# Attention and a mixture of experts in one program: a pick of the largest expert partly on GpSimd, two copies on ScalarE, clears later, one drain moved, rows turned in other steps

## The chip, the cores and the metric

The kernel runs on one core of a Trainium2 chip. Its time is the device time of one execution in microseconds (us). PE is TensorE, ACT ScalarE, DVE VectorE, POOL GpSimd, SP SyncE.

## The reference

`q`, `k`, `v` are 8 batches x 8 heads x 576 positions x 64. Heads 0 to 3 attend to the last 32 positions, heads 4 to 7 to every fourth of the last 128. The result, 4608 tokens of 512 numbers, goes through a mixture of 16 experts in 4 groups; a token belongs to one expert, its two softmax weights scale what the expert gives.

```python
attn = np.exp(scores - scores.max(-1)); attn /= attn.sum(-1) + 1e-9
x = np.matmul(attn, v).transpose(0, 2, 1, 3).reshape(4608, 512)
g_idx = np.argmax(x @ w_group, axis=1)          # group, then expert in it
e_idx = np.argmax(xg @ w_expert[g], axis=1)
h = np.maximum(xg[mask_e] @ w1[g, e], 0.0)      # 512 -> 1024
out[tok_idx] = combined[:, None] * (h @ w2[g, e])   # 1024 -> 512
```

## The kernel before

**Attention and routing.** The attention runs in 36 steps, each on 128 rows of `x` (two batches' share of 64 positions), as a pipeline over 40 loop steps `s`: scores of `s`, values (`av`, L339) and normalisation (L367, L371) of `s - 3`, transposes of `s - 4` for the gates. Values are needed in two places of partitions, so POOL copies half tiles of 64x1040 float32 (`shift_v`, L153 and L157: two a step, for the step after). Between these parts the loop spends a budget of time on a queue of routing work: `route(n)` for a pair of batches (nine steps each) finds each token's expert, its rank among the expert's tokens (`rk`, `slots`, `hl`), its softmax weight (sums on POOL, L462 to L468, then `val`, `parts`) and enters it in a table on PE (`bank`, from `mv`, L535 and L542). `base` holds the running count of tokens for each expert.

After the third and the fourth pair of batches (`AFTER = (2, 3)` indexes them from `base`) `pick(0)` and `pick(1)` choose the expert with the most tokens so far, by the index `ordi`, so that its weights can be loaded and three pieces of its work (EARLY) can begin inside the attention. A pick is seven or eight DVE operations: `cnt` (L585), `key`, (for the second: `key` less the first), `km`, `top`, `kk`, `km`, `ordi` (L607). SP reads `ordi` from memory (L959) and addresses the weights with it. Rows for the early pieces are gathered by POOL (L777) into `xe`, which is cleared first (L1060).

**Main loop.** After the attention there are 16 pieces of rows, sizes 186, 150, 368, 302, 300, 298, ..., 188. For a piece, `k` = 0 to 7 are the first layer's eight column blocks (L869 on PE; `hh` on ACT, L876; `hl` on DVE, L877: each value is split into two float16 numbers, and three products are added), `k` from 8 on the second layer's half tiles of up to 128 rows (L928; `yr` on ACT, L902, scattered by POOL, L889). The first layer writes `a` into four banks of PSUM in turn: block 4 of a piece waits until `hl` of block 0 has read its bank. All engines work in the order in which the loop is written. Within a step `k` that order is the step's own matmuls, `hh` and `hl`; then lists of later pieces (`LISTS`: rows of a piece from the table, L760 to L715); then gathers (`ask_ahead`, by `P2_ASKS` in piece 2; POOL, L801, four quarters for a tile of 128 rows); then the drain; then a turn; then a chunk of the weights of the piece after next (`split`: ACT `wh`, L681, DVE `wl`, L678).

A turn (`turner`) transposes one tile of gathered rows on DVE (`xt`, L822) and splits the one before into `xh` (ACT, L835) and `xl` (DVE, L836). It begins piece `j` only when the loop is one piece behind it, or two behind and past step 9, and a tile only LEAD = 6 steps after it was asked for. Turns come at odd `k` above 2. `xr` has five buffers.

**Drains.** `nc.gpsimd.drain()` (L1273) makes POOL wait for the transfers it has started; it stands in piece 2 at `k` = 12 and in each later piece at `k` = 5, 14 in all.

Of the kernel before, what the change touches and what calls it, by code (L numbers as in the profile page):

```python
# [8 lines left out]
F32 = mybir.dt.float32  # L9
# [4 lines left out]
ALU = mybir.AluOpType  # L14
AX = mybir.AxisListType
PSUM = bass.MemoryType.PSUM

P = 128
# [4 lines left out]
NE = 16  # L23
# [24 lines left out]
DEEP = 3  # L48
NXR = 5
LEAD = 6  # L50
P2_ASKS = (0, 2, 4, 6, 9, 11)
LISTS = {(1, 7): [3], (2, 4): [4], (2, 9): [5]}
NWST = 6
NWST2 = 1
BUDGET = (1.4, 1.4, 2.4, 1.8)
# [17 lines left out]
def moe_attention_kernel(ctx, tc, q, k, v, cmask, wgate, wpack, out):  # L73
# [76 lines left out]
    def shift_v(n):  # L150
        vs[n] = vp[n % NVS]
        odd, even = slice(0, 64), slice(64, P)
        nc.gpsimd.tensor_scalar(vs[n][even], vt[n][even], 1.0, 1.0, ALU.mult, ALU.mult)  # L153
        if n % NJ == 0:
            nc.gpsimd.memset(vs[n][odd], 0.0)
        else:
            nc.gpsimd.tensor_scalar(vs[n][odd], vt[n - 1][odd], 1.0, 1.0, ALU.mult, ALU.mult)  # L157
# [26 lines left out]
    pri = cp.tile([P, 4], F32, name="pri")  # L184
    base = [cp.tile([P, NE], F32, name="base0")] + [None] * NBP
    low = cp.tile([P, P], F32, name="low")
    iota = low[:, 0:MAXOV]
    oob = {4: cp.tile([P, 1], F32, name="oob4"), 2: cp.tile([P, 1], F32, name="oob2")}
    capt = cp.tile([P, NE], F32, name="capt")
# [17 lines left out]
    def iota_of(t, pattern, base, mult):  # L207
        nc.gpsimd.iota(t, pattern=pattern, base=base, channel_multiplier=mult, allow_small_or_imprecise_dtypes=True)

    def setup(part):  # L210
        if part == 0:
            nc.vector.memset(ones, 1.0)
            nc.gpsimd.affine_select(
                out=upper, in_=ones, pattern=[[1, P]], compare_op=ALU.is_gt, fill=0.0, base=0, channel_multiplier=-1
            )
            nc.sync.dma_start(wgr, wgate)
            iota_of(pri, [[-1, 4]], 4, 0)
            iota_of(base[0], [[REG, NE]], 0, 0)
            iota_of(low, [[1, P]], 0, 0)
        if part == 1:  # L220
            iota_of(high, [[REG // P, NE], [1, NK4]], 0, 0)
            nc.vector.tensor_scalar(high, high, float(P), HUGE, ALU.mult, ALU.add)
            nc.scalar.copy(high_ps, high.rearrange("p e k -> p (e k)"))
            nc.scalar.copy(pri_ps, pri)
            nc.vector.memset(E16, 0.0)
            nc.vector.memset(tab[:, 0], 0.0)
            nc.vector.memset(tab[:, 1], 2.0 * NTOK)
            nc.vector.memset(tab[:, 2], 2.0 * NTOK + 1.0)
            ids = wgr[:, 128:].rearrange("p (h v t) -> p h t v", h=2, v=2)
            nc.vector.tensor_copy(val[:, :, 1:3], ids[:, 0])  # L230
            nc.vector.tensor_copy(parts[:, :, 1:3], ids[:, 1])
        if part == 2:
            nc.gpsimd.memset(xe[0][0], 0.0)
            nc.sync.dma_start(xd[NTOK : NTOK + 1, :], xe[0][0][0:1, :])
        if part == 3:
            for j in range(4):
                nc.gpsimd.memset(odd[Q4 * j : Q4 * j + Q4], float(j % 2))
            for g, t in oob.items():
                for i in range(g):
                    nc.gpsimd.memset(t[P // g * i : P // g * i + P // g], float(g * NTOK + i))  # L240
            for r in range(NE):
                nc.vector.memset(capt[:, r : r + 1], float(CAPS[r]))
# [340 lines left out]
    def count(pairs):  # L583
        cnt = sm.tile([P, NE], F32, name="cnt")
        nc.vector.tensor_tensor(cnt, base[pairs], base[0], ALU.subtract)  # L585
        return cnt

    def pick(r):
        T = lambda nm, shape, dt=F32: sm.tile([P] + shape, dt, name=nm)
        cnt = count(AFTER[r])  # L590
        yield 0
        key = T("key", [NE])
        nc.vector.scalar_tensor_tensor(key, cnt, float(NE), iota[:, 0:NE], ALU.mult, ALU.subtract)
        yield 0
        for i in range(r):
            nc.vector.scalar_tensor_tensor(key, top[:, i], -float(NE * NTOK), key, ALU.mult, ALU.add)
            yield 0
        km, kk = T("km", [1]), T("kk", [NE])
        nc.vector.tensor_reduce(km, key, axis=AX.X, op=ALU.max)
        yield 0  # L600
        nc.vector.tensor_tensor(top[:, r], key, km.broadcast_to([P, NE]), ALU.is_equal)
        yield 0
        nc.vector.tensor_tensor(kk, top[:, r], iota[:, 0:NE], ALU.mult)
        yield 0
        nc.vector.tensor_reduce(km, kk, axis=AX.X, op=ALU.add)
        yield 0
        nc.vector.tensor_copy(ordi[:, r : r + 1], km)  # L607
        picked.append(r)
        yield 0

    def settle(i):
        r, off, n, pairs = EARLY[i]
# [369 lines left out]

    def early_slots():
        for i, (_, _, _, pairs) in enumerate(EARLY):
            while i not in found:
                yield
            for t in range(NET[i]):
                fetch_rows(xe[i][t], ente[i], t, pairs * TPB * P)
            yield
# [15 lines left out]
    for s in range(NT + 4):  # L1005
        ripe = bool(gate)
        step_now[0] = s
        if s < NT:
            scores(s)
        if 0 <= s - 3 < NT:  # L1010
            av(s - 3)
        if s < NT:
            softexp(s)
        if 0 <= s - 3 < NT:
            if ripe:
                gate.clear()
            normalise(s - 3)
        if start:
            n = start.pop()
            routes.append(route(n))  # L1020
            next(routes[-1])
            if len(routes) == 1:
                gate.append(1)
            for i, (_, _, _, pairs) in enumerate(EARLY):
                if pairs == n + 1:
                    routes.append(settle(i))
        left = spend(BUDGET[min(max(s - 4, 0) // NJ, NBP) - 1])
        if s % 2 == 0:
            load_q(s + 4)
        if s == 0:  # L1030
            load_k(4, 0)
        if s != 1:
            load_k(s + 4 - s % 2, s % 2 if s else 1)
        if s % 2 == 1 or s == 0:
            load_v(s + 2 + s % 2)
        if 0 <= s - 3 < NT:
            store(s - 3)
        if 0 <= s - 4 < NT:
            transpose_x(s - 4)
        if 0 <= s - 1 < NT:  # L1040
            transpose_p(s - 1)
        if left:
            spend(left)
        flush()
        if s < NT - 1:
            shift_v(s + 1)
        if 2 <= s <= 8 and s % 2 == 0:
            setup(s // 2 - 1)
        for r in picked:
            if r not in ev:  # L1050
                expert(r)
        if 0 in ev and not wq:
            wq.append(prefetch())
        if s == NT - 1:
            keep.close()
            fe = pool("fe", side="right", reuse_waits="tile")
            for i in range(1, len(EARLY)):
                xe[i] = [fe.tile([P, DM], F32, name=f"xe{i}{t}") for t in range(NET[i])]
                for t in xe[i]:
                    nc.gpsimd.memset(t, 0.0)  # L1060
            room = fe.tile([P, 48 * P], F16, name="room")
            cut = lambda a, c: room[:, a * P : (a + c) * P].rearrange("p (c n) -> p c n", c=c)
            for i in range(2):
                xs, hs_ = (cut(24 * i, 4), cut(24 * i + 4, 4)), (cut(24 * i + 8, 8), cut(24 * i + 16, 8))
                eb.append([early(i, xs, lambda hs_=hs_: hs_)])
        if eb:
            run(eb[0], EARLY_STEPS.get(s, 0))
        run(wq)
        if s >= 4 and (s - 4) % NJ == NJ - 1:
            bp = (s - 4) // NJ  # L1070
            if bp < NBP - 1:
                start.append(bp)
        run(eq)
    while routes:
        run(routes)
# [115 lines left out]
    def ask(n, got):  # L1191
        for _ in range(min(n, len(got[4]))):
            got[4].pop(0)()
            held_rows[0] += 1
            asked[id(got[2]), len(got[2]) - 1] = slot[0]

    def begin(got):
        ent, cs, xrs, tq, _ = got
# [46 lines left out]
    def turner():  # L1245
        def ripe(xrs, t):
            return len(xrs) > t and (now[2] or slot[0] >= asked[id(xrs), t] + LEAD)

        for j in range(1, len(pieces)):
            while len(known) <= j or j > now[0] + 1 and (j > now[0] + 2 or now[1] < 9):  # L1250
                yield
            got = begin(known[j])
            yield from spread_quarters(got[3], got[2], pieces[j][2], ripe)
            built[j] = got

    turn = [turner()]
    for i, (r, off, cap) in enumerate(pieces):
# [6 lines left out]
        for k, _ in enumerate(ffn(wsets[r % 2], xs, ent, cs, cap, new_h, tq=tq)):  # L1264
# [4 lines left out]
                    known_next(0)  # L1269
            if k in P2_ASKS if i == 2 else i > 2 and (k in (1, 3, 5) or k == 11 and nt(pieces[min(i + 3, NE - 1)][2]) > 2):  # L1270
                ask_ahead()
            if i > 1 and k == (12 if i == 2 else 5):
                nc.gpsimd.drain()  # L1273
            if k % 2 and k > 2:
                run(turn)
            k0, steps = (0, 8) if k < 8 else (8, 2 * nsel)
            if k == 0:
# [114 lines left out]
```

## Time and profile before

| | us |
|---|---|
| median of 3 runs (lowest, highest) | 573.03 (572.88, 574.16) |
| profiled execution, whole | 575.0 |
| its span on the core | 573.3 |
| PE busy | 541.6 (94%) |
| DVE busy | 428.3 (75%) |
| ACT busy | 331.7 (58%) |
| POOL busy | 325.4 (57%) |

A row of a timeline gives the start, the duration, the engine, the line, the operation with what it writes and reads, and in brackets how long the engine was idle before it and what ended that. In the windows view the number in brackets behind a busy time counts instructions, and PEclk is the share of PE's full clock that was granted. The profiled execution lies 1.7 us over its span and 2.0 us over the median.

### The profile page before, as it was taken

Reading aid. Unit: us, or ns where it says so; the run is one execution under the profiler, and the core shown is the slowest. Engines: PE = TensorE matmul, PEld = TensorE weight load, DVE = VectorE, ACT = ScalarE, POOL = GpSimd, SP = SyncE. Lnnn points to the kernel's source line nnn. Section 1 sums busy time; section 2 is a strip of 40 time slices with the busy share of each in tenths; the row PEclk is TensorE's granted clock in tenths of the full one; section 3 lists DMA queues with packets and bytes.
Section 4 is the critical chain, followed back from the end, with each engine's and each line's share of the span. In section 5 each row is a group of like instructions: output and inputs, shape, how many; then the busy total and the mean of one; then the engine's idle time right before and its main releaser. Section 6 shows DMA issues by size and latency. Waiting matters only on the chain.

```text
span 573.3 us, 16182 instructions
## 1 busy us (share of the span) xinstructions
PE 541.6 (94%) x6340; PEld 382.8 (67%) x6340; DVE 428.3 (75%) x870; ACT 331.7 (58%) x656; POOL 325.4 (57%) x332
## 2 busy tenths in 40 slices
PE   4999999898899999999997999999999999999995
PEld 2787877676767777554665566665756756766873
DVE  5775987889789916985958786978889879777710
ACT  7465685875856426845545456466765756755521
POOL 2795686645565861287476684574646646645011
PEclk9899999998999999999997999999999999999999
DMA  7999887994683453785656775857778678778110
GB/s 218 359 297 332 280 293 252 320 326 127 227 293 98 166 221 116 242 276 176 190 159 200 237 223 177 269 173 231 225 233 256 204 260 273 230 244 286 36 32 30
DMA packets 45824, 125.90 MB, mean 220 GB/s; under 512 B 7693, under 2 KB 8595, under 8 KB 45746
## 3 DMA queue, kind: packets, MB, share of 16 engines
q1 hardware_dynamic: 37506, 105.36, 56.7%
q0 software_dynamic: 8240, 19.48, 9.7%
q8 instruction: 51, 0.84, 0.6%
q14 instruction: 27, 0.22, 0.1%
HBM read 105.93 MB, written 19.22 MB: 218 GB/s over the span
## 4 chain that ended last, share of the span: by engine, by line
PE 57%; DVE 7%; issue 3%; POOL 2%; ACT 1%; DMA 1%; POOLq 0%; DVEq 0%; ACTq 0%
PE a L869 29%; PE y L928 28%; DVE wa2l L678 1%; DVE xt L822 1%; DVE hl L877 1%; DVE xl L836 1%; DMA xr<-xd,sentq 1%; POOL xe L777 1%; DVE wa1l L678 1%; POOL xr L801 1%; DVE wb1l L678 0%; PE pt L850 0%; ACT yr L902 0%; ACT off L270 0%; DVE mv L542 0%
## 5 line engine op out<-in xcount | busy, mean ns | idle before, releaser
L801 POOL DMA_INDIRECT xr<-xd,sentq x129 | 159.4, 1236 | 39.5 <-issue 33.6
L928 PEld LDWEIGHTS <-hh 128*128 128x128 f16 (+14 forms) x960 | 67.2, 99 | 61.5 <-issue 5.0
L889 POOL DMA_INDIRECT out<-yr,sent x30 | 34.2, 1141 | 113.8 <-ACT yr L902 28.4
L877 DVE SCALAR_TENSOR_TENSOR hl<-a,hh 128x256 f16<-128x256 f32 (+14 forms) x136 | 55.2, 420 | 33.3 <-ACT hh L876 33.1
L902 ACT ACTIVATE yr<-y,cs 128x512 f32<-128x512 f32 (+4 forms) x30 | 20.6, 687 | 100.1 <-PE y L928 54.3
L869 PE MATMUL a<-xh,wb1h 128*128 128x256 f16 (+7 forms) x288 | 76.7, 270 | 1.1 <-ACT xh L835 1.1
L869 PE MATMUL a<-xl,wb1h 128*128 128x256 f16 (+7 forms) x288 | 76.6, 270 | 0.2 <-DVE xl L836 0.2
L869 PE MATMUL a<-xh,wb1l 128*128 128x256 f16 (+7 forms) x288 | 76.6, 270 | 0.0
L876 ACT ACTIVATE hh<-a 128x256 f16<-128x256 f32 (+14 forms) x136 | 51.4, 382 | 41.2 <-PE a L869 40.3
L869 PE MATMUL a<-xh,wa1h 128*128 128x186 f16 (+7 forms) x256 | 72.1, 282 | 3.0 <-DVE hl L877 3.0
L869 PE MATMUL a<-xl,wa1h 128*128 128x186 f16 (+7 forms) x256 | 72.0, 282 | 0.3 <-DVE xl L836 0.3
L869 PE MATMUL a<-xh,wa1l 128*128 128x186 f16 (+7 forms) x256 | 71.9, 281 | 0.0
L869 PEld LDWEIGHTS <-wa1h 128*128 128x128 f16 x640 | 59.6, 99 | 15.6 <-issue 3.5
L869 PEld LDWEIGHTS <-wb1h 128*128 128x128 f16 x576 | 54.2, 98 | 11.0 <-issue 1.6
L928 PE MATMUL y<-wb2h,hl 128*128 128x512 f16 (+7 forms) x272 | 59.4, 304 | 1.1 <-DVE hl L877 1.1
L928 PE MATMUL y<-wb2h,hh 128*128 128x512 f16 (+7 forms) x272 | 59.5, 305 | 0.0
L928 PE MATMUL y<-wb2l,hh 128*128 128x512 f16 (+7 forms) x272 | 59.4, 304 | 0.0
L928 PE MATMUL y<-wa2h,hh 128*128 128x512 f16 (+7 forms) x208 | 56.7, 331 | 0.0
L928 PE MATMUL y<-wa2l,hh 128*128 128x512 f16 (+7 forms) x208 | 56.6, 330 | 0.0
L928 PE MATMUL y<-wa2h,hl 128*128 128x512 f16 (+7 forms) x208 | 56.6, 330 | 0.0
L153 POOL TENSOR_SCALAR vs<-v 64x1040 f32<-64x1040 f32 x36 | 38.7, 1088 | 30.5 <-DMA v<-v 18.2
L928 PEld LDWEIGHTS <-hl 128*128 128x128 f16 (+14 forms) x480 | 34.3, 99 | 28.7 <-DVE hl L877 2.0
(218 smaller groups left out, 1271.7 us busy)
## 6 DMA issues: line engine op xcount, KB each, us to landing
w<-wpack SPq DMA_DIRECT2D x128, 512.0 KB, 4.2
v<-v SPq DMA_DIRECT2D x36, 260.0 KB, 5.7
kr<-k SPq DMA_DIRECT2D x34, 256.0 KB, 5.6
qb<-q SPq DMA_DIRECT2D x17, 512.0 KB, 6.0
xd<-x SPq DMA_DIRECT2D x32, 256.0 KB, 4.4
xr<-xd,sentq POOLq DMA_INDIRECT x129, 4.7
xd<-x SPq DMA_DIRECT2D x8, 128.0 KB
qb<-q SPq DMA_DIRECT2D x2, 256.0 KB, 3.3
```

The source lines that it names most:

```text
L153: nc.gpsimd.tensor_scalar(vs[n][even], vt[n][even], 1.0, 1.0, ALU.mult, ALU.mult)
L678: nc.vector.scalar_tensor_tensor(l, staged.pop((r, i - 1)), SW, h, ALU.mult, ALU.subtract)
L777: nc.gpsimd.indirect_dma_start(out=xr[:, 256 * h : 256 * h + 256], out_offset=None, in_=xd[0:known].rearrange("n (h c) -> (n h) c", h=2), ...
L801: nc.gpsimd.indirect_dma_start(out=xr[:, T], out_offset=None, in_=xd.rearrange("n (g c) -> (n g) c", g=4), in_offset=bass.IndirectOffsetOn ...
L822: nc.vector.transpose(xt, xrs[t][:, 0:m].rearrange("p t (d c) -> p t c d", c=4))
L836: nc.vector.tensor_tensor(l, xt, h, ALU.subtract)
L869: nc.tensor.matmul(a[:, 0:cap], ww[:, c * FF + f * P : c * FF + f * P + P], xx[:, c, 0:cap], start=(i == 0), stop=(i == len(mm) - 1),)
L876: nc.scalar.activation(hh[:, f, 0:cap], a[:, 0:cap], AF.Relu)
L877: nc.vector.scalar_tensor_tensor(hl[:, f, 0:cap], a[:, 0:cap], 0.0, hh[:, f, 0:cap], ALU.max, ALU.subtract)
L889: ins = nc.gpsimd.indirect_dma_start(out=out.rearrange("n (g c) -> (n g) c", g=g), out_offset=bass.IndirectOffsetOnAxis(ap=at, axis=0), in ...
L902: nc.scalar.activation(yr[0:n, :], yp[0:n, :], AF.Copy, scale=cs[0:n, t : t + 1])
L928: nc.tensor.matmul(yp[P // g * j : P // g * j + n, 0 : DM // g], h[:, f, t * P : t * P + n], ww[:, f * DM + DM // g * j : f * DM + DM // g ...
```

## The change

The pick leaves out `cnt`: `key` is formed from `base` and a constant `origin` that POOL makes at setup. `kk` and the sum over it become six POOL operations (`place`), queued with the sums of the softmax (`posts`, run by `flush` at a step's end, or by `spend`). Values of steps 32 and 33 are copied by ACT, ahead of the exponential of the same step, not by POOL at the end of the step before. The clears of `xe` for the second and third early piece, and their gathers, come from step 37 on. In the main loop pieces 0 and 2 have turns in other steps, piece 2 may begin at step 8 of piece 0, and the tail row tile that is asked for at the very beginning counts as asked `LEAD` steps earlier; the lists of piece 3 come at step 6 of piece 0 and not at step 7 of piece 1. The drain of piece 2, step 12, goes to piece 1, step 2.

```diff
+TURNS = {0: (1, 3, 5, 8, 9, 10, 11), 2: (3, 5, 7, 8, 9, 10, 11, 12, 13)}
-LISTS = {(1, 7): [3], (2, 4): [4], (2, 9): [5]}
+VS_ACT = (32, 33)
+DRAINS = {1: 2}
+LISTS = {(0, 6): [3], (2, 4): [4], (2, 9): [5]}
...
+        if n in VS_ACT:
+            nc.scalar.copy(vs[n][even], vt[n][even])
+            nc.scalar.copy(vs[n][odd], vt[n - 1][odd])
+            return
...
+            nc.gpsimd.tensor_scalar(origin, base[0], float(NE), None, ALU.mult)
+            nc.gpsimd.tensor_tensor(origin, origin, iota[:, 0:NE], ALU.add)
...
-        cnt = count(AFTER[r])
-        nc.vector.scalar_tensor_tensor(key, cnt, float(NE), iota[:, 0:NE], ALU.mult, ALU.subtract)
+        nc.vector.scalar_tensor_tensor(key, base[AFTER[r]], float(NE), origin, ALU.mult, ALU.subtract)
...
-        nc.vector.tensor_tensor(kk, top[:, r], iota[:, 0:NE], ALU.mult)
-        nc.vector.tensor_reduce(km, kk, axis=AX.X, op=ALU.add)
-        nc.vector.tensor_copy(ordi[:, r : r + 1], km)
+        posts.append(lambda: place(r))
+    def place(r):
+        kk = sm.tile([P, NE], F32, name="kk")
+        nc.gpsimd.tensor_tensor(kk, top[:, r], iota[:, 0:NE], ALU.mult)
+        h = NE
+        while h > 1:
+            h //= 2
+            nc.gpsimd.tensor_tensor(kk[:, 0:h], kk[:, 0:h], kk[:, h : 2 * h], ALU.add)
+        nc.gpsimd.tensor_copy(ordi[:, r : r + 1], kk[:, 0:1])
...
-            while i not in found:
+            while i not in found or i and step_now[0] < NT + 1:
...
+        if s in VS_ACT:
+            shift_v(s)
-        if s < NT - 1:
+        if s < NT - 1 and s + 1 not in VS_ACT:
             shift_v(s + 1)
-                for t in xe[i]:
-                    nc.gpsimd.memset(t, 0.0)
+        if s == NT + 1:
+            for t in xe[1] + xe[2]:
+                nc.gpsimd.memset(t, 0.0)
...
-            asked[id(got[2]), len(got[2]) - 1] = slot[0]
+            asked[id(got[2]), len(got[2]) - 1] = slot[0] or -LEAD
-            while len(known) <= j or j > now[0] + 1 and (j > now[0] + 2 or now[1] < 9):
+            while len(known) <= j or j > now[0] + 1 and (j > now[0] + 2 or now[1] < (8 if j == 2 else 9)):
-            if i > 1 and k == (12 if i == 2 else 5):
+            if k == DRAINS.get(i, 5 if i > 2 else -1):
                 nc.gpsimd.drain()
-            if k % 2 and k > 2:
+            if k in TURNS.get(i, ()) or i not in TURNS and k % 2 and k > 2:
                 run(turn)
```

## Rows read from the trace of the kernel before

**Rows 1.** Windows: stretch, length, busy us (xinstructions) by engine, PEclk, DMA share, GB/s.

```profile
320.00:559.00 239.00, 239.00 (x2037) 164.00 (x2036) 183.84 (x315) 139.72 (x238) 127.10 (x102) 1.00 0.65 209
132.11:134.30 2.19, 2.19 (x41) 1.86 (x41) 1.75 (x7) 1.53 (x5) 1.78 (x2) 1.00 0.01 4
137.72:141.29 3.57, 3.57 (x41) 3.12 (x41) 3.54 (x5) 2.06 (x6) 3.24 (x6) 0.52 0.66 162
146.48:149.17 2.69, 1.43 (x37) 1.13 (x37) 0.64 (x2) 2.66 (x9) 2.69 (x7) 1.00 0.55 122
296.75:303.03 6.28, 6.28 (x51) 4.67 (x51) 2.27 (x3) 1.82 (x3) 2.88 (x3) 1.00 0.33 117
306.26:315.31 9.05, 9.05 (x49) 5.93 (x49) 7.50 (x17) 4.46 (x8) 7.15 (x7) 0.69 0.88 284
```

**Rows 2.** Waits of PE: line, releaser, us in total, times, longest us.

```profile
PE o L339 <- DVE x L371: 5.2, 6, 1.4
PE a L869 <- DVE hl L877: 3.0, 1, 3.0
...
PE o L339 <- DVE hl L509: 2.1, 1, 2.1
PE bank L561 <- POOL mv L535: 1.3, 1, 1.3
PE a L869 <- ACT xh L835: 1.1, 1, 1.1
PE y L928 <- DVE hl L877: 1.1, 2, 0.5
```

**Rows 3.** The line of the drains: duration ns min/median/max, first and last start.

```profile
L1273 POOLq DRAIN  x14: 3977/14164/16655, 267.8 to 551.5; - x14
```

**Rows 4.** Timeline of POOL, 258 to 310 us: start, us, operation, idle before it.

```profile
283.62 1.32 POOL L889 DMA_INDIRECT out<-yr,sent  x1 [6.23 <-ACT wa2h L681]
```

**Rows 5.** Chain of waits, 265 to 310 us: start, us, what.

```profile
296.64 3.99 DMA xr<-xd,sentq
```

**Rows 6.** Timeline of DVE, 258 to 310 us.

```profile
300.76 1.10 DVE L822 STREAM_TRANSPOSE xt<-xr 128x512 f32<-128x512 f32 x1 [5.29 <-DMA xr<-xd,sentq]
```

**Rows 7.** Timeline of ACT, 199 to 240 us.

```profile
221.07 0.69 ACT L902 ACTIVATE yr<-y,cs 128x512 f32<-128x512 f32 x1 [3.44 <-issue]
...
221.84 2.00 ACT L681 ACTIVATE wa1h<-w 128x1024 f16<-128x1024 f32 x2
...
225.90 0.48 ACT L876 ACTIVATE hh<-a 128x150 f16<-128x150 f32 x2
...
228.87 0.62 ACT L835 CAST xh<-xt 128x512 f16<-128x512 f32 x1
```

**Rows 8.** Timeline of DVE, 199 to 240 us.

```profile
226.60 0.54 DVE L877 SCALAR_TENSOR_TENSOR hl<-a,hh 128x150 f16<-128x150 f32 x2
```

**Rows 9.** Timeline of POOL, 199 to 242 us.

```profile
237.93 0.98 POOL L889 DMA_INDIRECT out<-yr,sent  x1 [11.88 <-DVE three L738]
```

**Rows 10.** Timeline of DVE, 125 to 150 us.

```profile
132.47 0.83 DVE L585 TENSOR_TENSOR cnt<-base,base 128x16 f32<-128x16 f32 x1 [0.27 <-ACT base L499]
...
134.22 0.17 DVE L603 TENSOR_TENSOR kk<-top,low 128x16 f32<-128x16 f32 x1
```

**Rows 11.** Timeline of POOL, 125 to 150 us.

```profile
132.23 1.05 POOL L153 TENSOR_SCALAR vs<-v 64x1040 f32<-64x1040 f32 x1 [5.08 <-DMA xe<-xd,ente]
...
141.42 0.20 POOL L467 TENSOR_TENSOR se<-sc 128x9 f32<-128x9 f32 x1
...
147.09 1.44 POOL L1060 MEMSET xe<- 128x512 f32 x3
148.51 1.17 POOL L535 TENSOR_TENSOR mv<-ohh,parts 128x256 f16<-128x256 f32 x2
```

**Rows 12.** Timeline of ACT, 125 to 150 us.

```profile
131.11 0.66 ACT L322 ACTIVATE p<-d 128x512 f32<-128x512 f32 x1 [2.14 <-DVE d L316]
```

**Rows 13.** Timeline of PE, 130.5 to 150 us.

```profile
133.81 0.60 PE L329 MATMUL t<-id,p 128*128 128x128 f32 x4
```

More of the change, by code (lines that the diff above doesn't have):

```diff
@@ L186, in moe_attention_kernel @@
     low = cp.tile([P, P], F32, name="low")
+    origin = cp.tile([P, NE], F32, name="origin")
     iota = low[:, 0:MAXOV]
@@ L589, in pick @@
         T = lambda nm, shape, dt=F32: sm.tile([P] + shape, dt, name=nm)
-        cnt = count(AFTER[r])
-        yield 0
-        key = T("key", [NE])
-        nc.vector.scalar_tensor_tensor(key, cnt, float(NE), iota[:, 0:NE], ALU.mult, ALU.subtract)
+        key, km = T("key", [NE]), T("km", [1])
+        nc.vector.scalar_tensor_tensor(key, base[AFTER[r]], float(NE), origin, ALU.mult, ALU.subtract)
         yield 0
@@ L597, in pick @@
             yield 0
-        km, kk = T("km", [1]), T("kk", [NE])
         nc.vector.tensor_reduce(km, key, axis=AX.X, op=ALU.max)
@@ L601, in pick @@
         nc.vector.tensor_tensor(top[:, r], key, km.broadcast_to([P, NE]), ALU.is_equal)
+        posts.append(lambda: place(r))
         yield 0
-        nc.vector.tensor_tensor(kk, top[:, r], iota[:, 0:NE], ALU.mult)
-        yield 0
-        nc.vector.tensor_reduce(km, kk, axis=AX.X, op=ALU.add)
-        yield 0
-        nc.vector.tensor_copy(ordi[:, r : r + 1], km)
+    def place(r):
[6 more added lines that the diff above has]
+        nc.gpsimd.tensor_copy(ordi[:, r : r + 1], kk[:, 0:1])
         picked.append(r)
-        yield 0
     def settle(i):
```

## The prediction

> **What bounds the kernel now.** I read the windows view first. PE is the bound: from 320 to 559 us it is busy in all of the 239.00 us [rows 1], and no other engine comes near. So a change can only take away what PE idles before that stretch, and the time at half its clock, and what is saved there is kept to the end, because after 320 us PE waits for nobody. The waits of PE come second [rows 2]: 3.0 us in the main loop for `hl`, 1.1 for `xh`, twice about 0.55 for `hl` in the second layer; in the attention 2.1 us for `hl` (L509), 1.3 for the table (`bank` after `mv`), and six waits of at most 1.4 us for `x`. The windows around the two longest show the third thing. The 41 matmuls after the 2.08 us wait took 3.57 us at a granted clock of 0.52; the same 41 of the step before took 2.19 at 1.00. A first layer after the 3.02 us wait took 9.05 us at 0.69, where the stretch with as many matmuls ahead of that wait took 6.28 at 1.00. So a long wait of PE here costs itself and then 1.4 or 2.8 us more at the lower of the two levels (1.2 and not 2.4 GHz). After the wait of 1.42 us at 146.48 the clock stayed at 1.00 [rows 1]. The timelines come last, for each wait in turn: who is late, and what it stood behind.
>
> **The drain.** The 3.02 us wait ended at 306.26 with `hl` of piece 4, and DVE was late with that because, in its written order, it stood before `xt` of piece 5 from 295.47 to 300.76, idle 5.29 us [rows 6]. The rows it waited for came by a gather issued at 296.64 that took 3.99 us to land, at 300.63 [rows 5]. That gather is one of a row of gathers that POOL issues nearly without a pause from 283.62 on, and before 283.62 POOL sat idle for 6.23 us [rows 4]: that is where the drain of piece 2, step 12, stands (the drains' first start is 267.8 [rows 3]). The scatter behind it used rows that had been ready long before. With the drain gone POOL goes on at 277.39, up to 6.2 us sooner, and the rows land at 294.4. DVE comes there at 295.47, so its wait goes with 1.1 us to spare, and PE needs only 3.02 of the 5.29 us. Term: 3.0 and 2.8 us of clock, **-5.8**. Nothing that the gathers need is late: their lists are made by step 9 of piece 2, and the buffers of `xr` come free with transposes of piece 3 and the first of piece 4, long written by then.
>
> Where the drain goes, in piece 1, step 2 (about 224 us), POOL has nothing to do: its next instruction is at 237.93 after 11.88 us idle [rows 9]. Behind it stand that scatter and piece 3's gathers. The 14 drains took 4.0 to 16.7 us, 14.2 in the middle [rows 3], most of that with gathers queued ahead; here one or two scatters are ahead. I take 0; the upper bound (16.7 us, to 241) would make the scatter 3 us late, which I treat under the rivals.
>
> **Turns sooner, pieces 0 and 2.** In piece 2 the turns at 7, 8, 9, 10, ... bring `xh` and `xl` of piece 3 ahead of the last `yr` on ACT; before, they stood behind it. The 1.1 us wait for `xh` at the start of piece 3 goes: **-1.1**. DVE will stand waiting in the same piece for rows that have not landed at step 8, but PE needs nothing from it there: all `hl` of piece 2 are done by then.
>
> In piece 0 the transposes and halves of piece 2 (three `xt`, 1.10 us each as at 300.76 [rows 6], and three `xl`) and the lists of piece 3 leave piece 1, where DVE was full and PE waited twice for `hl`: **-1.1**. They go to the second half of piece 0, where DVE has room. But ACT has them in order too. With turns at 8, 9, 10, 11 the three `xh` are written behind steps 9, 10 and 11, so all of them behind `yr`, which waits for PE and runs at 221.07 [rows 7]. In before ACT did after it a short `xh`, three chunks of weights (two took 2.00 us) and two tail outputs, and came to `hh` of piece 1, block 0, at 225.90; `hl` followed at 226.60 [rows 8]. Now three `xh` of 0.62 us [rows 7] replace the short one, 1.9 us for some 0.2 (an estimate: a quarter of the columns, a third of 0.62): `hh` comes 1.7 us later, `hl` too. Block 4 writes the bank that this `hl` frees; PE took block 4 up right behind it in before, with no slack. So a new wait: **+1.7** (1.4 if the `xh` overlap by 0.1 each as ACT's rows do; 2.3 if DVE's chunks push `hl` further by half a chunk). It lies between 1.42 us, after which the clock stayed, and 2.08, after which 1.4 us were lost, so I add half of that: **+0.7**.
>
> **The attention.** `pick(1)` on DVE loses `cnt`, 0.83 us, and `kk`, `km`, `ordi`, 0.17 each by `kk` [rows 10]: 1.3 us in all. They lie directly ahead of the 2.08 us wait, so it would shrink to some 0.7, below 1.42, and the 1.4 us of clock after it go as well. The rule that speaks against the size of this: the Trainium skill, SBUF — State Buffer, section Who interferes with whom, says that a DVE instruction with two inputs in SBUF and a GpSimd instruction that reads SBUF exclude each other. The trace agrees: `cnt` ended at 133.30, POOL's copy at 133.28 [rows 10, 11], and `kk` of the same size took 0.17. By that rule the wait of 0.66 us passes to `key`, which now has two inputs in SBUF, if POOL copies at that moment, and this term would be 0.7 and not 1.3, and with the half that I count below the forecast 0.3 us higher.
>
> The six POOL operations of `place` cost 0.20 us each by the adds of the softmax [rows 11], 1.2 us a pick and the pauses between them. POOL has them free: at 132.23 it had been idle for 5.08 us. SP reads `ordi` after them; the copies that stood there are gone, so I take 0 (bounds 0 and 1.2 a pick).
>
> The copies on ACT: the trace has no 64x1040 float32 copy on ACT. The nearest rows are 1.0 us for 128x1024 (two in 2.00) and 0.69 for 128x512 with a float32 result [rows 7], which doubled is 1.4 us. So 2.1 to 2.8 us a step, ahead of the exponential `p`. ACT was idle 2.14 us before `p` at 131.11 [rows 12], and the transposes that need `p` began at 133.81 [rows 13], 2.0 us after it ended. I take 0; with no cover it would be 2.1 a step. On POOL the copies had waited 5.08 us for a gather to land [rows 11], and the sums, `mv` and the table came late behind them. The clears (1.44 us) stood directly ahead of `mv` at 148.51, for which PE waited 1.3 us [rows 2, 11]; with both gone so should be that wait.
>
> That is 1.3 + 1.4 + 1.3 = 4.0 us at most. But PE waits for `x` in six other places, 5.2 us together [rows 2], so DVE is nearly full here, and the routing and the weights' halves all come one step sooner into it. What is saved in one step is likely to be waited for in the next. I take half, **-2.0** (ends -4.0 and 0).
>
> **Sum:** -5.8 - 1.1 - 1.1 + 1.7 + 0.7 - 2.0 = -7.6. From the profiled execution's 575.0 that is 567.4. The median lies 2.0 us under the profiled execution, so I forecast **565.4** as median against 573.03, 1.3% faster. 0.2% of this kernel (1.15 us) is about what a measurement can tell from none.
>
> **Rivals.**
> - *The attention gives it all.* -4.0 and not -2.0, and no loss of clock in piece 1: 565.4 - 2.0 - 0.7 = 562.7. For it: the waits named end with exactly the operations removed. Against: six waits for `x` beside them. Chance 0.15.
> - *The wait only moves.* In piece 1 2.3 us and the full 1.4 of clock, in the attention 0: 565.4 + 0.6 + 0.7 + 2.0 = 568.7. For it: ACT's order in piece 0 as worked out. Chance 0.15.
> - *The drain's gain does not come:* POOL's gathers wait for something else in that stretch (buffers, lists), `xt` still stands until about 300, the 3.0 and the 2.8 us remain: 571.2. Against: POOL's idle stretch of 6.23 us ends just after the drain and nothing else stands there. Chance 0.08.
> - *Slower: the drain blocks where it now stands.* If it waits for more than the last scatters, POOL's stream from 237.93 on starts late, and with it the gathers of pieces 3, 4 and 5, one behind the other. The 6.2 us gained at 277 take up the lateness: 1.1 us are spare before DVE waits, 2.3 more (5.29 less 3.02) before PE does. So from an end of the drain at 237.9 + 3.4 = 241.3 each us goes to PE. To lose the 7.6 us and 1.4 more it would have to end at 250.3, 26 us after its start, against at most 16.7 seen [rows 3, 9]: 574.4. Chance 0.04.
> - My forecast, 564 to 567: 0.58.
>
> Range: from 561.7 (the first rival less 1.0 for a shorter wait in piece 1) to 569.7 (the second and 1.0 for the copies on ACT); the last two rivals lie outside. Faster by more than 0.2%: 0.91 (all but the slow rival and half of the third); within 0.2%: 0.05; slower: 0.04.
>
> **What would show it.** Right: no wait of PE of 3 us near 300 and a granted clock of 1.00 there; no drain between 240 and 290 and POOL without a pause of 6 us; no `xh` wait at the start of piece 3; a wait of 1.4 to 2.3 us for `hl` in piece 1 at its fifth block; `cnt` gone, and the 2.08 us wait under 1.42 without the 0.52 window. Wrong: `xt` of piece 5 still waiting some 5 us; ACT's copies ending after 133 with PE waiting for `p`; a half clock at a new place, above all where a wait of 2 us or more arises, which would take back 1.4 to 2.8 us each.

## The result and the profile after

The changed kernel took 565.68 us (4 runs, 564.63 to 566.65) against 572.95 of the kernel before: ratio 0.9871, 95% interval 0.9829 to 0.9913. In a later series it was 565.29 against 572.69, 0.9868 (0.9826 to 0.9910). The forecast was 565.4 (561.7 to 569.7). The experiments were run in four series. In two of them the kernel before took 584 to 588 us, and each profiled execution has PE idle for 6 to 16 us that the profile puts to no wait; the times of these two, called the disturbed series below, are given, but carry no part of the account.

The profiled execution took 566.15 us, its span is 564.4, 8.86 less than that of before. Where the time went can be read from PE's timeline: the starts of the first matmul of each piece's first layer (and of DVE's `x` of step 20, which comes before both picks; of the change only the 0.5 us of POOL that make `origin` lie ahead of it), taken from the timelines of the two kernels and subtracted.

| stretch | before, us | after, us | difference |
|---|---|---|---|
| start to `x` of step 20 | 93.21 | 92.56 | -0.65 |
| to piece 0 (the rest of the attention) | 114.43 | 112.16 | -2.27 |
| piece 0 | 16.01 | 16.01 | 0.00 |
| piece 1 | 14.66 | 16.70 | +2.04 |
| piece 2 | 32.27 | 30.51 | -1.76 |
| piece 3 | 26.17 | 25.83 | -0.34 |
| piece 4 | 31.59 | 25.76 | -5.83 |
| all behind it | 244.94 | 244.89 | -0.05 |

The sum is -8.86. The first row is a spread between executions: it lay between -2.0 and +1.2 in the undisturbed ones profiled below, so that medians and not single executions tell the total.

The windows of after that answer to [rows 1] (stretch, length, busy by engine, PEclk, DMA share, GB/s):

```profile
136.46:140.10 3.64, 3.64 (x52) 2.78 (x55) 3.44 (x9) 3.30 (x11) 3.06 (x5) 0.67 0.86 249
225.90:230.00 4.10, 4.05 (x38) 4.05 (x38) 3.87 (x8) 2.33 (x6) 0.00 (x0) 0.58 0.91 304
293.85:300.20 6.35, 6.35 (x53) 4.72 (x52) 6.05 (x13) 4.35 (x8) 3.98 (x4) 1.00 0.82 257
320.00:550.00 230.00, 230.00 (x1956) 158.63 (x1956) 177.73 (x308) 134.18 (x231) 125.27 (x100) 1.00 0.67 212
```

The stretch at the start of piece 4 now takes 6.35 us at 1.00, where the first layer took 9.05 at 0.69; PE still never idles behind 320. Two stretches stand at 0.67 and 0.58 of the clock, both at the lower of the two levels for a part of them: one in the attention, where before had 0.52 behind its wait of 2.08 us, and a new one in piece 1. They follow the two longest waits that PE has behind the first loads, in the list that answers to [rows 2]:

```profile
PE o L349 <- DVE val L525: 2.9, 1, 2.9
...
PE a L880 <- DVE hl L888: 1.8, 1, 1.8
PE bank L571 <- ACT den L359: 1.5, 2, 1.2
PE bank L571 <- ACT ohl L281: 1.0, 1, 1.0
PE tx L410 <- DVE x L381: 0.8, 1, 0.8
PE o L349 <- DVE x L381: 0.8, 2, 0.6
```

The 3.0 us wait for `hl` of piece 4 and the 1.1 for `xh` are gone, and so is the wait for `mv`. Of the waits for `x`, 5.2 us in before, 0.8 are left, and the transposes (`tx`) now wait 0.8 for it. A wait of 1.8 us for `hl` is new; it is the one that the prediction set at 1.7.

POOL, to be laid beside [rows 4, 9], then the drains as in [rows 3], the first of them by itself below, then DVE where piece 5's rows are transposed, as in [rows 6]:

```profile
237.05 0.98 POOL L900 DMA_INDIRECT out<-yr,sent  x1 [12.25 <-ACT yr L913]
...
275.71 1.02 POOL L900 DMA_INDIRECT out<-yr,sent  x1 [0.30 <-ACT csq L737]
277.04 1.39 POOL L812 DMA_INDIRECT xr<-xd,sentq  x1 [0.30 <-issue]
```

```profile
L1287 POOLq DRAIN  x14: 3966/13322/14715, 222.6 to 542.7; - x14
L1287 POOLq DRAIN  x1: 7034/7034/7034, 222.6 to 222.6; - x1
```

```profile
290.62 1.18 DVE L689 SCALAR_TENSOR_TENSOR wb1l<-w,wb1h 128x1024 f16<-128x1024 f32 x1
291.72 1.11 DVE L833 STREAM_TRANSPOSE xt<-xr 128x512 f32<-128x512 f32 x1
```

Between 258 and 291 POOL now runs with 0.3 us between instructions; the first drain stands at 222.6 and was over after 7.03 us, at 229.7, and POOL's next instruction, at 237.05, waited for `yr` and not for it. (Of the signs one fails by the letter: a drain does start before 290, at 283.8. It is piece 3's, at 292.5 in before.) `xt` at 291.72 begins right behind the chunk of weights, with no wait.

### The profile page after: what moved, and what is told of

Same layout as the page of the kernel before. It is cut to its first block, busy times and chain, and to the rows that moved or that the text cites. A ratio compares the mean times of both kernels' runs of the same rounds, so it can differ in the third digit from the quotient of the medians.

```text
span 564.4 us, 16183 instructions
## 1 busy us (share of the span) xinstructions
PE 538.6 (95%) x6340; PEld 384.0 (68%) x6340; DVE 425.4 (75%) x862; ACT 336.1 (60%) x660; POOL 323.6 (57%) x342
## 4 chain that ended last, share of the span: by engine, by line
PE 66%; issue 2%; DVE 2%; ACT 1%; POOL 0%; POOLq 0%; DVEq 0%
PE a L880 32%; PE y L939 32%; PE lt_ps L424 0%; DVE wa1l L689 0%; PE pt L861 0%; DVE mv L552 0%; PE rp L734 0%; POOL out L900 0%; DVE xl L847 0%; DVE wb1l L689 0%; DVE wa2l L689 0%; DVE xt L833 0%; ACT off L280 0%; DVE x L381 0%; DVE room L888 0%
## 5 line engine op out<-in xcount | busy, mean ns | idle before, releaser
L812 POOL DMA_INDIRECT xr<-xd,sentq x129 | 161.2, 1250 | 39.5 <-issue 33.9
L880 PE MATMUL a<-xh,wb1h 128*128 128x256 f16 (+7 forms) x288 | 77.9, 273 | 1.8 <-DVE hl L888 1.8
L880 PE MATMUL a<-xh,wb1l 128*128 128x256 f16 (+7 forms) x288 | 77.8, 273 | 0.0
L880 PE MATMUL a<-xl,wb1h 128*128 128x256 f16 (+7 forms) x288 | 77.8, 273 | 0.0
L880 PE MATMUL a<-xh,wa1h 128*128 128x186 f16 (+7 forms) x256 | 70.8, 277 | 0.0
L880 PE MATMUL a<-xh,wa1l 128*128 128x186 f16 (+7 forms) x256 | 70.7, 277 | 0.0
L880 PE MATMUL a<-xl,wa1h 128*128 128x186 f16 (+7 forms) x256 | 70.7, 277 | 0.0
L160 POOL TENSOR_SCALAR vs<-v 64x1040 f32<-64x1040 f32 x34 | 35.6, 1060 | 24.0 <-DMA v<-v 18.3
```

The lines of the kernel that those rows point to most:

```text
L812: nc.gpsimd.indirect_dma_start(out=xr[:, T], out_offset=None, in_=xd.rearrange("n (g c) -> (n g) c", g=4), in_offset=bass.IndirectOffsetOn ...
L880: nc.tensor.matmul(a[:, 0:cap], ww[:, c * FF + f * P : c * FF + f * P + P], xx[:, c, 0:cap], start=(i == 0), stop=(i == len(mm) - 1),)
```

## The experiments

Theory A held that the terms are separate, each in the place where PE's timeline changed. Theory B, in each run, is what would have to be so if it is not. All times by stretch are taken as in the table above.

**The drain alone.** The kernel before with this and nothing else:

```diff
+DRAINS = {1: 2}
-            if i > 1 and k == (12 if i == 2 else 5):
+            if k == DRAINS.get(i, 5 if i > 2 else -1):
```

> The kernel before with only the drain moved, on a chip on which the profile shows no unnamed idle of PE. Theory A (terms apart, each where PE's timeline changed): the 3.0 us wait near 306 and the half clock after it go, 5.8 us: ratio to before 0.990, the waits of piece 1 and of 1.1 us at piece 3 stay. Theory B (the gathers come in time only with the turns of piece 2): a ratio of 0.997 or more, with xt of piece 5 still waiting.

568.96 us against 573.00, ratio 0.9915 (0.9882 to 0.9948). Piece 4 took 25.76 us, as in the changed kernel, and 31.59 in before: 5.83 us, so the drain needs none of the other edits. The median gained 4.0 (3.0 to 6.8 by the interval, which holds 5.8 and shuts out theory B's 0.997). The profiled execution was the longest of its seven (575.11, the others 567.61 to 569.75): in it piece 2 and the start of piece 3 lost 4.6 us. The chain of waits (start, us, what) shows how:

```profile
267.71 6.13 DMA out<-yr,sent
...
273.95 0.69 ACT yr L903
```

`yr` had to wait for a scatter that lay 6.13 us in flight, since `yr` has only two buffers, and `xh` of piece 3 stands behind `yr` on ACT in the old order. The run with turns and lists back, below, has the same main loop, and its execution lost nothing there (32.27 and 26.17 us, as in before). Whether the other executions of the drain alone lost part of this too their times alone don't tell, so the 1.8 us between trace and median stay open.

The first go at this kernel, in a disturbed series, gave 597.05 against 587.82, ratio 1.0115 (1.0032 to 1.0199), with 11.9 us of unnamed idle of PE in its profile:

> The kernel before with only the drain moved. Theory A (the terms are separate, each lies where PE's timeline changed): the 3.0 us wait of PE near 306 and the half clock after it go, 5.8 us, so about 567.2 against 573.0; the waits in piece 1 (0.5, 0.5, 0.3) and of 1.1 at piece 3 stay. Theory B (the gathers come in time only because the turns of piece 2 let DVE and the row buffers go sooner): xt of piece 5 still waits 3 us or more and the time is 570 or over.

In the same series the drain alone was put back in the changed kernel (`DRAINS = {2: 12}`):

> The changed kernel with the drain where it was. Theory A: the wait of some 3 us at the start of piece 4 and the half clock come back, 565.7 + 5.8 = 571.5. Theory B (the turns of piece 2 alone would have brought piece 5's rows in time, the drain's place being no matter): within 1 us of the changed kernel.

596.52 against 587.82, 1.0201 (1.0133 to 1.0268): slower than before, which neither theory says. The wait at the start of piece 4 was only 0.4 us there, as PE itself came late. It decides nothing.

**No drain ahead of piece 3** (`DRAINS = {}` and `5 if i > 2 else -1` alone):

> The changed kernel without any drain before piece 3. Theory A (the drain costs nothing in piece 1): no difference over 0.5 us, POOL's scatter after it and the gathers of piece 3 start at the same time. Theory B (it holds POOL up): the gathers of piece 3 start 1 us or more sooner and the time falls by up to 1 us.

590.23 against 584.32, ratio 1.0095 (1.0051 to 1.0140), in the other disturbed series: the changed kernel itself was not run in it, so this time decides nothing. That the drain costs nothing in piece 1 rests on the rows above (it ends 7.4 us before POOL's next instruction) and on the next run: with the drain in piece 1 and the old turns, pieces 1, 2 and 3 took what they took in before.

**Turns and lists back.** The changed kernel with these lines as they were:

```diff
-TURNS = {0: (1, 3, 5, 8, 9, 10, 11), 2: (3, 5, 7, 8, 9, 10, 11, 12, 13)}
+TURNS = {}
-LISTS = {(0, 6): [3], (2, 4): [4], (2, 9): [5]}
+LISTS = {(1, 7): [3], (2, 4): [4], (2, 9): [5]}
-            asked[id(got[2]), len(got[2]) - 1] = slot[0] or -LEAD
+            asked[id(got[2]), len(got[2]) - 1] = slot[0]
```

and `now[1] < 9` for all pieces.

> The changed kernel with turns, lists and the begin of piece 2 as they were. Theory A (piece 1 lost what pieces 2 and 3 gained): the wait of 1.76 us and the half clock there go, the old waits come back, the ratio to before stays within 0.0015 of 0.987. Theory B (the turns gained on the whole): 0.990 or more.

566.89 against 573.00, ratio 0.9882 (0.9850 to 0.9915): not told apart from the changed kernel. Piece by piece it was before again: 14.66, 32.27, 26.17, and piece 4 25.75. PE's waits from 200 to 330 us:

```profile
PE a L880 <- ACT xh L846: 1.1, 1, 1.1
PE y L939 <- DVE hl L888: 1.1, 2, 0.5
PE a L880 <- DVE xl L847: 0.5, 2, 0.3
```

These are the waits of before, without the 3.0 us one. So turns and lists together give +2.04 - 1.76 - 0.34 = -0.06 us: nothing. The first go, beside the first one of the drain alone:

> The changed kernel with turns, lists and the begin of piece 2 as they were. Theory A: the new wait of 1.76 us and its half clock in piece 1 go (-3.4), the old waits there, at piece 2 and at piece 3 come back (+1.4 + 0.5 + 1.6), net 0: 565 to 566.5. Theory B (the turns also help the drain's gain or later pieces): 567.5 or more. Theory C (without the piece 1 wait the rest is kept): 563.5.

602.22 against 587.82, ratio 1.0292 (1.0214 to 1.0370). In that execution PE stood idle for 9.0 us ahead of piece 3; `yr` and `xh` on ACT started late with no wait named (in that profile a wait for a transfer could not be named, see the last section).

**Two of the three `xh` ahead of `yr`.** The changed kernel with piece 2's rows turned sooner:

```diff
-TURNS = {0: (1, 3, 5, 8, 9, 10, 11), ...
+TURNS = {0: (1, 3, 5, 6, 7, 8, 9), ...
-LISTS = {(0, 6): [3], ...
+LISTS = {(0, 8): [3], ...
-... now[1] < (8 if j == 2 else 9)):
+... now[1] < (6 if j == 2 else 9)):
```

> The kernel with piece 2's rows turned at steps 6 to 9 of piece 0, once more, beside the changed kernel on the same chip. Theory A (piece 1's wait and its half clock are gone): 2.5 to 3.4 us under the changed kernel. Theory B (the gain of piece 1 is waited for elsewhere before piece 4): less than 1 us under it.

562.74 against 572.69, ratio 0.9828 (0.9779 to 0.9876), beside the changed kernel's second measurement in the same series:

> The changed kernel itself once more, as the measure for the other runs of this series, in which the kernel before took 584 to 588 us and not 573. Theory A (the gain belongs to the change): the same ratio to before as at first, 0.983 to 0.991. Theory B (where PE stands idle for reasons that the profile doesn't name, the gain is lost in those): a ratio of 1.00 or more, with such idle times of several us in the profile between 200 and 310.

565.29, 0.9868. Piece 1 took 13.25 us and not 16.70, the other pieces the same to 0.01: 3.45 us by the traces, 2.55 by the medians of four runs each (the intervals of the two ratios overlap). ACT of the changed kernel at the end of piece 0 first, to be laid beside [rows 7], and its DVE, to be laid beside [rows 8]; then ACT and DVE of this one, then this one's window of piece 1:

```profile
218.14 0.69 ACT L913 ACTIVATE yr<-y,cs 128x512 f32<-128x512 f32 x1 [3.96 <-issue]
218.73 0.61 ACT L846 CAST xh<-xt 128x512 f16<-128x512 f32 x1
...
220.19 0.60 ACT L846 CAST xh<-xt 128x512 f16<-128x512 f32 x1
...
222.62 0.62 ACT L846 CAST xh<-xt 128x512 f16<-128x512 f32 x1
...
224.22 0.48 ACT L887 ACTIVATE hh<-a 128x150 f16<-128x150 f32 x2
```

```profile
223.86 0.67 DVE L847 TENSOR_TENSOR xl<-xt,xh 128x512 f16<-128x512 f32 x1
224.47 1.21 DVE L689 SCALAR_TENSOR_TENSOR wa1l<-w,wa1h 128x1024 f16<-128x1024 f32 x1
225.60 0.52 DVE L888 SCALAR_TENSOR_TENSOR hl<-a,hh 128x150 f16<-128x150 f32 x2
```

```profile
214.34 0.62 ACT L846 CAST xh<-xt 128x512 f16<-128x512 f32 x1 [0.52 <-DVE xt L833]
215.55 0.62 ACT L846 CAST xh<-xt 128x512 f16<-128x512 f32 x1 [0.59 <-DVE xt L833]
...
218.72 0.69 ACT L913 ACTIVATE yr<-y,cs 128x512 f32<-128x512 f32 x1 [1.60 <-issue]
...
223.76 0.48 ACT L887 ACTIVATE hh<-a 128x150 f16<-128x150 f32 x2
```

```profile
224.09 0.54 DVE L888 SCALAR_TENSOR_TENSOR hl<-a,hh 128x150 f16<-128x150 f32 x2
```

```profile
226.00:230.00 4.00, 4.00 (x42) 2.82 (x40) 3.76 (x8) 3.70 (x9) 0.00 (x0) 1.00 0.97 339
```

In the changed kernel three `xh` follow `yr`, and from `yr` to `hh` of piece 1 it takes 6.08 us (4.83 in before). Here two come at 214.34 and 215.55, where ACT has nothing to do, and it takes 5.04; PE waits for nobody from 200 to 330 us, and the clock stays at 1.00. Theory A holds for the time and for `hh`, which comes 1.04 us sooner behind `yr`. But PE waits for `hl`, and from `yr` to `hl` it takes 7.46 us in the changed kernel, 5.53 in before and 5.37 here: 2.09 us sooner, of which ACT's order gives 1.04. The rest is DVE's, where in the changed kernel an `xl` and a chunk of weights run from 223.86 to 225.68 ahead of `hl`; the same edit moved `xt`, `xl` and the lists too, so the run does not part ACT from DVE. This kernel has the lowest median of the study. Its first go:

> The changed kernel with the turns of piece 0 at 1, 3, 5, 6, 7, 8, 9 (piece 2 may begin at 6) and the lists of piece 3 at step 8, so that two of the three xh are written ahead of yr on ACT. Theory A (piece 1's wait of 1.76 us and its half clock come from the three xh behind yr): hh of piece 1 comes 1.0 us sooner, the wait at its fifth block shrinks under 0.8 and the clock there stays at 1.00, 2.5 to 3.4 us gained on the changed kernel. Theory B (DVE's transposes and weights are what hl waits for, ACT's order is no matter): hl at the same time, the wait stays at 1.4 or more, no gain.

592.25 against 584.32, ratio 1.0097 (1.0046 to 1.0148): the wait in piece 1 was gone there too, but PE had lost more than that by then, unnamed.

**The attention back.** The changed kernel with `pick`, copies and clears as in before:

> The changed kernel with pick, copies and clears as they were. Theory A (the attention's edits give 2.3 us): ratio 0.987 + 0.004 = 0.991, and PE reaches the first layer of piece 0 some 2.3 us later against its step 20. Theory B (only the spread of loads between executions): within 0.001 of 0.987.

568.01 against 573.00, ratio 0.9920 (0.9892 to 0.9948). From `x` of step 20 to piece 0 it took 114.61 us; before took 114.43 and the drain alone, also with the old attention, 114.62. With the new one it took 112.16 and 112.74 in two executions of the changed kernel, 112.17 with turns and lists back and 111.97 with the turns sooner. So the attention's edits are worth 1.7 to 2.6 us by the traces, 2.3 in the mean, and 2.8 to 3.0 by the ratios (0.0049 and 0.0052 of 573), whose intervals overlap. Its first go:

> The changed kernel with pick, copies and clears as they were. Theory A: the attention gave 2.3 us (PE was 0.66 us ahead at step 20 and 2.92 ahead at its end), so 565.7 + 2.3 = 568.0. Theory B (all 2.9 us that PE is ahead at the attention's end belong to these edits): 568.6. Theory C (the lead at the attention's end is the spread of the loads between executions): within 0.7 us of the changed kernel, and its own profile shows the end of the attention as early.

586.92 against 587.82, ratio 1.0003 (0.9960 to 1.0045).

The run showed two things more. The first lies in the attention. PE's longest wait there was 2.15 us (2.08 in before, at the same matmul), and this time the clock stayed at 1.00 behind it. The window has the 41 matmuls that took 3.57 us at 0.52 in before [rows 1]; then come PE's values of the next step, here and in before:

```profile
137.90:140.09 2.19, 2.19 (x41) 1.74 (x41) 2.19 (x3) 1.96 (x5) 2.19 (x2) 1.00 0.48 98
```

```profile
142.42 0.38 PE L346 MATMUL o<-vs,pt 128*32 128x130 f32 x2 [1.18 <-DVE val L522]
```

```profile
142.50 0.27 PE L339 MATMUL o<-vs,pt 128*32 128x130 f32 x1
```

Counted from `x` of step 20 these values began after 49.13 us here and after 49.29 in before: PE waited 1.18 us for DVE where before had no wait. So of the 1.4 us at the lower clock the full clock gave back 0.16, in one execution of each.

The second lies in piece 1, which has the same wait of 1.8 us for `hl` as the changed kernel (waits, then the window behind it):

```profile
PE a L876 <- DVE hl L884: 1.8, 1, 1.8
```

```profile
229.00:233.00 4.00, 3.87 (x52) 3.51 (x52) 3.76 (x9) 2.24 (x6) 0.00 (x0) 1.00 0.92 311
```

Piece 1 took 15.08 us and not 16.70: the clock stayed at 1.00 behind the same wait. So the +2.04 of piece 1 comes apart: 15.08 less the 13.25 of the run without the wait is 1.83 for the wait, 16.70 less 15.08 is 1.62 for the clock, and 13.25 less the 14.66 of before is -1.41 for what left piece 1.

**Chunks later.** The kernel with two of the three `xh` ahead of `yr`, with the weight chunks of the first expert one attention step later:

```diff
-SPLITS = (2, 0, 2, 2, 2, 2, 2, 1, 1, 1, 1)
+SPLITS = (3, 0, 2, 2, 2, 2, 2, 1, 1, 1, 1)
```

> The kernel with piece 2's rows turned at steps 6 to 9 of piece 0 (ratio 0.983 before), with the weight chunks of the first expert one attention step later. Theory A (in the changed kernel the wait of 2.9 us at step 33 is DVE's backlog: the chunk of 1.2 us that fell into the step of the second pick): the wait falls to some 1.8 us and the lower clock after it goes, 1 to 2.5 us gained, ratio 0.979 to 0.981. Theory B (the chunk is only waited for in the next step): ratio 0.982 to 0.984, the wait of step 33 smaller, that of step 32 or 34 larger.

565.09 against 573.00, ratio 0.9851 (0.9816 to 0.9886). From step 20 to piece 0 it took 114.68 us, where the same kernel without this line took 111.97: as much as the attention had gained is gone, the pieces are as they were. ACT's first chunk began at 110.44 and not 106.85 (111.66 in before). PE's waits from 93 to 205 us, and the window behind the longest:

```profile
PE o L349 <- DVE x L381: 4.7, 3, 2.8
PE o L349 <- DVE val L525: 1.3, 1, 1.3
```

```profile
142.01:145.50 3.49, 3.13 (x47) 2.59 (x48) 2.92 (x7) 2.89 (x8) 0.98 (x2) 0.65 0.00 0
```

The wait of step 33 did fall, from 3.0 to 1.3 us, more than theory A has it. But a wait of 2.8 us for `x` two steps on took its place, with the clock at 0.65 behind it, and waits for `x` came back that the changed kernel doesn't have. So the chunk is what made the wait of step 33 long, as theory A has it, and the time went as theory B has it or worse: 2.7 us lost by the traces of one execution each, 1.3 by the ratios, which stand in different series and whose intervals overlap.

## Why the prediction was right, and where not

**The drain: right in mechanism and size.** -5.8 forecast, -5.83 measured, the same to 0.01 in every kernel of the undisturbed series that has it. Its cost at the new place is 0, as taken. The slow rival (the drain blocks) and the third (the gain doesn't come) are out.

**Turns: right in mechanism, two sizes off, near in sum.** Pieces 2 and 3 gave 1.76 + 0.34 = 2.1 and not 1.1. The wait for `xh` at the start of piece 3 gave 1.28; the rest is two shorter waits for `xl` at the second matmul of piece 2 (0.32, in the timelines 0.48) and of piece 3 (0.17, in the timelines 0.33), which I had left out of the rows. Piece 1 was forecast at -1.1 + 1.7 + 0.7 = +1.3 and came to -1.41 + 1.83 + 1.62 = +2.04. The wait was sized well, though not for the reason in its working: counted from `yr`, `hh` came 1.25 us later and not 1.7, and `hl` 1.93, since DVE's `xl` and chunk pushed it by another 0.68. The working had that push only as its upper end; that the two errors meet near 1.7 is luck. The step that failed is the half of the clock's cost: it is a cost that comes whole or not at all, and the mean of the two is the time of no execution. Turns and lists as a whole gave -0.06 against the +0.2 forecast, so this edit brought nothing, and with the turns two steps sooner piece 1 is 3.45 us shorter (2.55 by the medians).

**The attention: the sum right by luck, the step wrong.** -2.0 forecast, -2.27 and -1.7 in two executions of the changed kernel. But the step "it would shrink to some 0.7, below 1.42, and the 1.4 us of clock after it go as well" failed: the wait of 2.08 us grew to 2.94 (it is put down to `val`, the operation right behind `x`), and the clock fell behind it as before. Nor was the 1.4 us there to be had: in the run with the old attention the clock stayed, and PE was 0.16 us ahead one step later. Of the three parts of the 4.0 only the 1.3 for `mv` came as worked out. DVE of the changed kernel in that step, then POOL:

```profile
130.37 0.18 DVE L601 SCALAR_TENSOR_TENSOR key<-base,origin 128x16 f32<-128x16 f32 x1 [0.63 <-ACT base L509]
130.58 0.91 DVE L604 SCALAR_TENSOR_TENSOR key<-top,key 128x16 f32<-128x16 f32 x1
...
132.86 1.22 DVE L689 SCALAR_TENSOR_TENSOR wa1l<-w,wa1h 128x1024 f16<-128x1024 f32 x1
134.00 0.68 DVE L325 TENSOR_REDUCE mx<-s 128x8 f32<-128x512 f32 x1
...
135.62 0.69 DVE L381 TENSOR_TENSOR x<-o,den 128x512 f32<-128x512 f32 x1
```

```profile
130.39 1.08 POOL L164 TENSOR_SCALAR vs<-v 64x1040 f32<-64x1040 f32 x1
...
132.28 2.12 POOL L618 TENSOR_TENSOR kk<-kk 128x8 f32<-128x8 f32 x4
```

`cnt`, `kk`, its sum and `ordi` are gone from DVE, and still `x` comes late: a chunk of weights (1.22 us at 132.86) now stands in this step ahead of `mx`, and the second `key` took 0.91 us beside POOL's copy, which ended at 131.47, `key` at 131.49. The Trainium skill, SBUF — State Buffer, section Who interferes with whom, says that a DVE instruction with two inputs in SBUF contends with a GpSimd instruction that reads SBUF. The trace agrees, so the wait of `cnt` did pass on, though not to the `key` that the prediction named: the first one, begun 0.02 us before the copy, took 0.18. The chunk is there because the first expert is known sooner: ACT's first chunk began at 106.06 and not 111.66. I had named that (weights' halves one step sooner) as the reason to halve the term, and did not place the chunk in a step. (The picks come after the second and the third pair of batches, as `base[2]` and `base[3]` count them, one pair sooner than the section on the kernel before says.)

Where the 2.27 us come from in its place: in before the values (`o`) waited four times, 4.0 us, for `x` between 93 and 205, in the changed kernel 0.2 (1.1 in its second execution), and `tx` 0.8; the 1.3 for `mv` went, and 1.2 and 1.0 for the table came in. With the chunks one step later as much is lost, with all three edits in place. So the steps that the chunks fall into are worth as much as all the edits together; that the edits gain by nothing else is not shown. That it is the pick's shorter chain that moves the chunks follows from the code; which of the three edits in the attention is worth what by itself was not tried.

**The copies on ACT** cost nothing, as taken:

```profile
127.53 1.06 ACT L157 COPY vs<-v 64x1040 f32<-64x1040 f32 x1
...
129.57 0.70 ACT L332 ACTIVATE p<-d 128x512 f32<-128x512 f32 x1
```

Each took 1.06 us, near the lower bound, and `p` started right behind them; no wait of PE names `p`. PE waited 0.25 us at 131.19 for `xT`, which also stands behind them on ACT, but that lies ahead of the 2.94 us wait, which takes it up.

**The rivals.** The second (the wait only moves, with the full clock) is what happened in piece 1, and the attention's grew too; it did not bring 568.7, because the drain's and the attention's terms came in full. The profiled execution gained 8.86 us and the medians 7.3; the one of before lay 2.0 us over its median, the one of the changed kernel 0.5. A part of the near hit on 565.4 is luck: the errors, +0.7 in piece 1 and -1.0 at pieces 2 and 3, offset each other, and the attention's -2.0 is half of a sum of which two parts did not come.

## What to carry to other kernels

Where an engine works in written order, look for what a moved operation comes to stand in front of, on every engine that it uses: two of three `xh` in an idle stretch of ACT and not behind `yr`, with their `xt` and `xl` on DVE, made piece 1 3.45 us shorter. A wait for a queue's end belongs where that queue is idle and nothing follows soon; moved so, it was the largest part here, and the only one whose gain was the same in every undisturbed execution. When a chain gets shorter, ask which other work starts sooner for it and into which step it falls: one step for the chunks was worth as much here as all that the attention had gained. And time at a lower clock is worth something only where PE would not wait for another engine next: 1.6 us in piece 1, 0.16 in the old attention.

## What the runs showed of the hardware that was not expected

The same wait of PE, 1.76 us before the same matmul, was followed by a granted clock of 0.58 in the changed kernel, in both of its profiled executions at 0.62 or less, and of 1.00 in the kernel with the old attention. In that kernel the wait of 2.15 us in the attention was followed by 1.00 too, where before had 0.52 behind 2.08 us. So between these lengths the wait alone doesn't tell whether the clock falls, and that it costs 1.4 us wherever it falls, as the prediction had it, doesn't hold: the price was 1.6 us in piece 1 and 0.16 in the old attention.

In two series, on two chips, PE stood idle for 6 to 16 us in each profiled execution with nothing named that it waited for; in the other two such idle came to less than 1. The six profiles of these two series have no landing time for any transfer (in the other eight the chunks of weights, for one, have a median of 4.2 to 5.5 us from issue to landing), so in them a wait for a transfer can't be named: idle without a name is not shown there to be idle without a cause. With turns and lists back, for one, ACT stood idle for 5.86 and 7.18 us before two `yr` of piece 2, unnamed, where in the drain alone a `yr` waited 6.04 us for a scatter. Whether it is the same is not shown. The parts' gains were not found again there, and each change but one came out slower than before. What PE's idle is stays open, and so does what the change is worth under it.
